# Loading batch 0 in 1 KB pieces and batch 1 ahead of the weights, with queries left in piece order

## The chip, the cores and the metric

One core of one Trainium2 chip. The metric is the device time of one execution in microseconds (us). The kernel before takes 378.52 us, the median of 3 runs (378.29 to 378.92). "Faster" and "slower" need 2%.

## The reference

```python
# q, k, v: 8 batches x 8 heads x 576 rows x 64 columns, fp32; s: 8 x 8 x 576
scores = scale * q @ k.T
bias   = -(cum[..., :, None] - cum[..., None, :])        # cum = cumsum(max(s, 0))
scores = where(causal, -1e9, scores + minimum(bias, 0))
x      = softmax(scores) @ v            # heads side by side: 8 x 576 x 512
xn     = (x - mean) / sqrt(var + 1e-6) * g_ln
out    = x + maximum(xn @ w_ch1, 0) @ w_ch2              # 512 -> 2048 -> 512
```

## The kernel before

A hand-scheduled loop over 64 heads. Head g's scores, exponentials and products with v lie beside the transposes of later heads and beside pieces ("units") of the MLP of an earlier batch. The parts that matter here:

```python
QUADS = (1, 2)                 # batches whose q and k are loaded in 1 KB pieces
ypool = ctx.enter_context(tc.tile_pool(name="ypool", bufs=2))   # output tiles yo
...
def head_in(what, b, h, eng):          # loads of batches 0 to 2, one head each
    o, i = homes[what, b][:, h, 0:NF, :], src[what][b, h, 0 : NF * P, :]
    if b in QUADS and what != "v":     # partition p gets rows 4p to 4p+3: 1 KB
        eng.dma_start(out=o.rearrange("p t d -> p (t d)"),
                      in_=i.rearrange("(p t) d -> p (t d)", t=NF))
    else:                              # partition p gets rows p, 128+p, ...: 4 x 256 B
        eng.dma_start(out=o, in_=i.rearrange("(t p) d -> p t d", p=P))
...
def t_quads(b, h, engs):               # transposes on TensorE, then a copy out of PSUM
    ...                                # that puts the columns back in row order, q and k
        copy(engs[i], qkT[b][0:DK, i * H + h, 0 : NF * P].rearrange("r (p t) -> r p t", t=NF),
             pts[i][0:DK, 0 : NF * P].rearrange("r (t p) -> r p t", t=NF))
...
late.append((out[c, a * P : (a + 1) * P, :], yo))      # a store of 128 rows x 2 KB
...
for c, g in enumerate((6, 6, 7, 7)):             at(g, "a", lambda c=c: load_w1(c))
for h, g in enumerate((0, 0, 1, 1, 7, 7, 8, 8)): at(g, "e", lambda h=h: b1_in(h))
for i, g in enumerate((10, 10, 11, 11)):         at(g, "b", lambda i=i: load_w2(i))
```

From batch 3 on, q and k are transposed by DMA instead (`t_dma`, tile qkT: 25 transposes, a median of 5.5 us from issue to landing in the kernel before). The page counts the packets of all queues as shares of 16 DMA engines: 63.5% of the span for queue q1, with the loads, 6.3% for q10, with most of the stores.

The softmax here doesn't subtract the row's maximum and nothing guards it: scores larger than these inputs give would overflow.

Of the kernel before, what the change touches and what calls it, by code (L numbers as in the profile page):

```python
# [9 lines left out]
F32 = mybir.dt.float32  # L10
BF16 = mybir.dt.bfloat16
# [5 lines left out]
def kernel(  # L17
# [35 lines left out]

    QUADS = (1, 2)
    NPX = 2
# [17 lines left out]

    negm = const.tile([P, P], BF16, name="negm")
    nc.gpsimd.memset(negm, 0.0)
    nc.gpsimd.affine_select(
        out=negm, in_=negm, compare_op=ALU.is_ge, fill=-131072.0, base=0, pattern=[[1, P]],
        channel_multiplier=-1,
    )

# [16 lines left out]
    xnT_tail = const.tile([P, 2, KD, P], BF16, name="xnT_tail")  # L97

    scr = xbufs[0]
    ident_f = scr[:BH, 4:5, 64 : 64 + BH].rearrange("p a b -> p (a b)")  # L100
# [4 lines left out]

    nc.sync.dma_start(out=s_sb, in_=s.rearrange("b h s -> (b h) s"))


# [12 lines left out]
    def copy(eng, o, i):  # L121
        if eng == "act":
            nc.scalar.copy(out=o, in_=i)
        elif eng == "dve":
            nc.vector.tensor_copy(out=o, in_=i)  # L125
        else:
            nc.gpsimd.tensor_copy(out=o, in_=i)  # L127
# [33 lines left out]
    def t_quads(b, h, engs):  # L161
        pts = [ps_m.tile([P, 2 * 512], BF16, name="pt", tag="pm") for _ in range(2)]
        tails = pts[1][0:DK, NF * P : NF * P + 2 * P].rearrange("r (j n) -> r j n", j=2)
        for i in range(2):
            for p in range(NF):
                nc.tensor.transpose(  # L166
                    pts[i][0:DK, p * P : (p + 1) * P], aug[:, p, i * H + h, 0:DK], ident
                )
            nc.tensor.transpose(tails[:, i, :], aug[:, NF, i * H + h, 0:DK], ident)
            copy(  # L170
                engs[i],
                qkT[b][0:DK, i * H + h, 0 : NF * P].rearrange("r (p t) -> r p t", t=NF),
                pts[i][0:DK, 0 : NF * P].rearrange("r (t p) -> r p t", t=NF),
            )
        copy(
            "dve", qkT[b][0:DK, :, NF * P : S].rearrange("r (j h) n -> r j h n", j=2)[:, :, h, :],
            tails[:, :, 0:TL],
        )

    def t_pe(b, h, engs=("dve", "dve")):  # L180
        if b in QUADS:
            return t_quads(b, h, engs)
        for j, eng in ((h, engs[0]), (H + h, engs[1])):
            pt = ps_m.tile([P, 2 * 512], BF16, name="pt", tag="pm")
            for p in range(NT):
                nc.tensor.transpose(pt[0:DK, p * P : (p + 1) * P], aug[:, p, j, 0:DK], ident)  # L186
            copy(eng, qkT[b][0:DK, j, :], pt[0:DK, 0:SP_])

# [9 lines left out]
    def score_mms(g):  # L198
        b, h = g // H, g % H
        s01 = ps_s.tile([P, 1024], F32, name="s01", tag="s01")  # L200
        s23 = ps_s.tile([P, 512], F32, name="s23", tag="s23")
        pot = ps_o.tile([P, 512], F32, name="pot", tag="pot")
        pots[g] = (pot, s01, s23)

        def mm(o, kb, lo, hi):
            lhsT = qkT[b][0:DK, H + h, kb * P : (kb + 1) * P]
            w = 0
            if g < NPM and lo == kb * P:
                w = min(P, hi - lo)
                nc.tensor.matmul(  # L210
                    o[:, 0:w], lhsT=lhsT, rhs=qkT[b][0:DK, h, lo : lo + w], start=True, stop=False
                )
                nc.tensor.matmul(
                    o[:, 0:w], lhsT=ident, rhs=negm[:, 0:w], start=False, stop=True
                )
            if lo + w < hi:
                nc.tensor.matmul(  # L217
                    o[:, w:], lhsT=lhsT, rhs=qkT[b][0:DK, h, lo + w : hi], start=True, stop=True
                )

        mm(s01[:, 0:512], 0, 0, 512)
        mm(s01[:, 512:576], 0, 512, 576)
        mm(s01[:, 576:1024], 1, 128, 576)
        mm(s23[:, 0:320], 2, 256, 576)
        mm(s23[:, 320:512], 3, 384, 576)
        mm(pot[:, 448:512], 4, 512, 576)

    def score_exp(g, part):
        pot, s01, s23 = pots[g]
        e = ebufs[g % 3]  # L230

        def ex(o, i):
            nc.scalar.activation(out=o, in_=i, func=ACT.Exp, scale=scale)  # L233

        def mask(d):
            nc.gpsimd.affine_select(  # L236
                out=d, in_=d, compare_op=ALU.is_ge, fill=0.0, base=0,
                pattern=[[0, d.shape[1]], [1, P]], channel_multiplier=-1,
            )

        if part == 0:
            ex(e[:, 0:1024], s01)
        else:
            ex(e[:, EO[2] : EO[2] + 512], s23)
            ex(e[:, EO[4] : EO[4] + TL], pot[:, 448:512])
            if g >= NPM:
                mask(e[:, 0 : 3 * S].rearrange("p (n c) -> p n c", c=S)[:, :, 0:P])
                mask(
                    e[:, EO[4] + P - 448 : EO[3] + P]
                    .rearrange("p (n c) -> p n c", c=448)[:, :, 448 - P : 448]  # L250
                )

# [39 lines left out]
    def store(c, a, yo):  # L292
        if c >= B:
            b0 = 4 * (c - B) + 2 * a
            late.append((out[b0, NF * P : S, :], yo[0:TL]))
            late.append((out[b0 + 1, NF * P : S, :], yo[TL:P]))
        else:
            late.append((out[c, a * P : (a + 1) * P, :], yo))

# [190 lines left out]
    def spin(n):  # L490
        for _ in range(n):
            nc.tensor.matmul(idle[:, 0:P], lhsT=ident, rhs=ident, start=True, stop=True)

    spin(44)
    nc.vector.tensor_scalar(
# [5 lines left out]
    )  # L501
    pc = ps_m.tile([P, 512], F32, name="pc", tag="pm")
    for p in range(NT):
        nc.tensor.transpose(pc[:, p * BH : (p + 1) * BH], cum[:, p * P : (p + 1) * P], ident_f)
    c8, r8 = (
        x[:, 0 : NT * BH].rearrange("p (t c) -> p t c", c=BH) for x in (xts[2], xts[1])
    )
    pc_v = pc[:, 0 : NT * BH].rearrange("p (t c) -> p t c", c=BH)

# [11 lines left out]
    cast_head("k", 0, 0, "pool")  # L521
    split(0, H, nc.vector, pc_v[:, :, 0:H], aug[:, :, H:HD, D1:DK])
    nc.scalar.activation(
# [3 lines left out]
    cast_head("k", 0, 1, "pool")  # L527
    spin(8)
    t_pe(0, 0, ("act", "dve"))
    nc.scalar.copy(out=c8, in_=pc_v)  # L530

    def cum_quads():

        pq = ps_m.tile([P, 512], F32, name="pq", tag="pm")[:, 0 : NF * 3 * H]
        pq = pq.rearrange("p (t c) -> p t c", t=NF)
        cum_q = cum[0 : 3 * H, 0 : NF * P].rearrange("c (p t) -> c t p", t=NF)
        for p in range(NF):
            nc.tensor.transpose(pq[:, p, :], cum_q[:, p, :], ident_f[0 : 3 * H, 0 : 3 * H])
        qs = slice(QUADS[0] * H, (QUADS[-1] + 1) * H)
        nc.vector.tensor_copy(out=c8[:, 0:NF, qs], in_=pq[:, :, qs])  # L540

# [10 lines left out]
    def at(g, pos, f):  # L552
        hooks.setdefault((g, pos), []).append(f)
# [13 lines left out]
    def t_next(g):  # L567
        t_pe((g + 2) // H, (g + 2) % H, ("dve", "act" if g >= H else "dve"))

    at(0, "a2", lambda: t_pe(0, 1))  # L570
    at(0, "a2", cum_quads)
    at(2, "c", lambda: split(H, 2 * H, nc.vector))
# [3 lines left out]
    for g in range(2 * H):  # L576
        if g < 12:
            at(g, "a", lambda g=g: feed(g))
        if g < 14:
            at(g, "a2" if g < H else "b", lambda g=g: t_next(g))  # L580
    for c, g in enumerate((6, 6, 7, 7)):
        at(g, "a", lambda c=c: load_w1(c))

    def heads_in(b, hs):
        for h in hs:
            for what in "qkv":
                head_in(what, b, h, nc.sync)

    def b1_in(h):
        if h == 2:  # L590
            nc.sync.dma_start(out=gln_b, in_=moe_g_ln.partition_broadcast(P))
        heads_in(1, (h,))
        if h % HH == 0:
            for what in "qkv":
                tails_in(what, 1, nc.sync, slice(h, h + HH))

    for h, g in enumerate((0, 0, 1, 1, 7, 7, 8, 8)):
        at(g, "e", lambda h=h: b1_in(h))
# [6 lines left out]
    def t_act(b, h):  # L605
        t_pe(b, h, ("dve", "act"))

# [18 lines left out]
    at(10, "c", lambda: chunk_units(0))  # L626
    for i, g in enumerate((10, 10, 11, 11)):
        at(g, "b", lambda i=i: load_w2(i))
    for p in (1, 2, 3, 4):
        at(6 + p, "e", lambda p=p: nc.gpsimd.memset(aug[:, p, :, DK:P], 0.0))  # L630


    def b2_in(g):
        if g == 12:
            for what in "qkv":
                tails_in(what, 2, nc.sync)
        heads_in(2, range(3 * (g - 12), min(H, 3 * (g - 12) + 3)))

    for g in (12, 13, 14):
        at(g, "a", lambda g=g: b2_in(g))  # L640
# [62 lines left out]
    for g in range(NG + 4):  # L703
# [7 lines left out]
        if g < NG:  # L711
            score_mms(g)
            run(g, "a2")
            score_exp(g, 0)
        mlp(min(1, nu))
# [44 lines left out]
```

## Time and profile before

| kernel before | value |
|---|---|
| time, median | 378.52 us |
| span of the profiled execution (its own time was 380.23 us) | 378.5 us |
| idle time of TensorE from 98.8 to 320 us | 0.8 us (221.20 less 220.41) |
| data of one store of batches 0 to 2, first packet to last, median of 12 (range) | 1.4 us (0.8 to 2.6) |

```profile
DVE x L273 <- DMA out_dram<-yo: 0.5, 1, 0.5
```

### The profile page before, as it was taken

The numbers are of one execution on the slowest core, as the hardware profiler recorded it, in microseconds if no ns is written. First come the engines' busy times: TensorE is split into PE (matmuls) and PEld (weight loads), VectorE is DVE, ScalarE is ACT, GpSimd is POOL, SyncE is SP. The second block draws the span as 40 slices with busy tenths as digits, with TensorE's granted clock in tenths as the row PEclk, the third lists the DMA queues.
The fourth block names the chain that finished last, engine by engine and source line by source line (L and its number), as shares of the span: only waits on it lengthen the run. The fifth ranks groups of instructions, "written<-read, shape, count | busy, mean of one in ns | idle before, by whom it ended". The sixth has DMA issues, their size and how long they took to land.

```text
span 378.5 us, 7931 instructions
## 1 busy us (share of the span) xinstructions
PE 354.7 (94%) x3017; PEld 204.5 (54%) x3017; DVE 201.9 (53%) x466; ACT 163.9 (43%) x295; POOL 167.6 (44%) x328
## 2 busy tenths in 40 slices
PE   6987878888999999999999999999999999899994
PEld 5966645455555455545555755555555555344471
DVE  6788575765454544594447435733555353933131
ACT  3755755154563457335632546444623554031020
POOL 3537964493634545575455544463444111500000
PEclk9998999999999999999999999999999999999998
DMA  9958989997999789999999999599804001420202
GB/s 164 207 150 190 221 143 187 245 248 176 176 227 227 137 198 211 229 198 205 174 210 239 174 246 224 119 195 207 156 29 113 29 2 55 113 55 0 86 28 55
DMA packets 175253, 59.12 MB, mean 156 GB/s; under 512 B 162224, under 2 KB 170416, under 8 KB 175216
## 3 DMA queue, kind: packets, MB, share of 16 engines
q1 hardware_dynamic: 165200, 46.43, 63.5%
q0 software_dynamic: 4224, 4.19, 7.0%
q10 hardware_dynamic: 5792, 8.00, 6.3%
q8 instruction: 23, 0.38, 0.4%
q14 instruction: 14, 0.11, 0.1%
HBM read 37.11 MB, written 9.44 MB: 123 GB/s over the span
## 4 chain that ended last, share of the span: by engine, by line
PE 75%; DMA 11%; DVE 6%; SPq 4%; issue 2%; POOL 1%; ACT 0%; DVEq 0%; POOLq 0%; ACTq 0%
PE ph L373 29%; PE py L384 28%; PE s L217 9%; PE pot L264 6%; DMA ring<-in_q_dram 4%; DMA ring<-in_v_dram 4%; DVE xn L323 2%; SPq L430 2%; DMA ring<-in_k_dram 1%; DVE stats L308 1%; DMA xnT<-xn 1%; SPq L422 1%; SPq L434 1%; DVE x L273 1%; PE pt L186 1%
## 5 line engine op out<-in xcount | busy, mean ns | idle before, releaser
L233 ACT ACTIVATE e<-s 128x1024 bf16<-128x1024 f32 (+1 forms) x128 | 99.0, 808 | 88.0 <-PE s L217 86.2
L384 PE MATMUL py<-w_bf,hT 128*128 128x512 bf16 x576 | 133.4, 379 | 0.0
L373 PE MATMUL ph<-xnT,w_bf 128*128 128x512 bf16 x512 | 120.7, 379 | 1.7 <-DMA xnT<-xn 1.7
L236 POOL TENSOR_SCALAR_AFFINE_SELECT e<-e 128x384 bf16<-128x384 bf16 x104 | 45.7, 464 | 111.2 <-ACT e L233 102.6
L358 DVE TENSOR_SCALAR hT<-ph 128x512 bf16<-128x512 f32 x72 | 49.6, 690 | 77.0 <-PE ph L373 76.4
L373 PEld LDWEIGHTS <-w_bf 128*128 128x128 bf16 x640 | 58.2, 98 | 50.3 <-issue 2.2
L384 PEld LDWEIGHTS <-hT 128*128 128x128 bf16 x576 | 53.1, 98 | 56.1 <-DVE hT L358 0.2
L356 ACT ACTIVATE hT<-ph 128x512 bf16<-128x512 f32 x72 | 43.0, 597 | 79.6 <-PE ph L373 77.3
L217 PE MATMUL s<-qkT 68*128 68x64 bf16 (+5 forms) x320 | 54.5, 287 | 0.0
L127 POOL CAST aug<-ring 128x512 bf16<-128x512 f32 (+2 forms) x85 | 44.4, 547 | 15.0 <-DMA ring<-in_k_dram 7.3
L390 DVE SCALAR_TENSOR_TENSOR yo<-py,rstd,x 128x512 f32<-128x512 f32 x32 | 24.0, 749 | 47.7 <-PE py L384 45.5
L217 PEld LDWEIGHTS <-qkT 68*128 68x128 bf16 x372 | 32.5, 98 | 24.7
L264 PEld LDWEIGHTS <-e 128*128 128x128 bf16 x960 | 37.9, 98 | 13.6 <-POOL e L236 1.1
L264 PE MATMUL pot<-v_bf,e 128*128 128x65 bf16 x960 | 40.1, 194 | 1.4 <-POOL e L236 1.0
L273 DVE TENSOR_TENSOR x<-pot,rinv 128x320 f32<-128x320 f32 x64 | 31.5, 492 | 2.9 <-DMA out_dram<-yo 0.5
L125 DVE COPY qkT<-pt 68x512 bf16<-68x512 bf16 (+2 forms) x49 | 21.9, 468 | 12.5 <-PE pt L166 4.4
L308 DVE BATCH_NORM_STATS2 stats<-x 128x6 f32<-128x256 f32 (+2 forms) x68 | 23.4, 398 | 0.3
L323 DVE SCALAR_TENSOR_TENSOR xn<-x,mv,gln_b 128x512 bf16<-128x512 f32 x32 | 23.2, 766 | 0.0
L127 POOL CAST v_bf<-ring 128x512 bf16<-128x512 f32 (+2 forms) x33 | 19.5, 613 | 2.2 <-DMA ring<-in_v_dram 2.2
L272 DVE RECIPROCAL rinv<-pot 128x5 f32<-128x5 f32 x64 | 12.0, 187 | 15.0 <-PE pot L264 14.9
L329 POOL TENSOR_TENSOR rstd<-rstd,nhalf 128x2 f32<-128x2 f32 x18 | 18.6, 1031 | 1.5
L166 PE MATMUL pt<-ident,aug 128*68 128x128 bf16 x128 | 11.8, 226 | 6.8 <-POOL aug L127 3.1
(78 smaller groups left out, 217.8 us busy)
## 6 DMA issues: line engine op xcount, KB each, us to landing
out_dram<-yo ACTq DMA_DIRECT2D x27, 256.0 KB, 3.3
ring<-in_q_dram SPq DMA_DIRECT2D x20, 256.0 KB, 4.9
ring<-in_k_dram SPq DMA_DIRECT2D x20, 256.0 KB, 4.8
ring<-in_v_dram SPq DMA_DIRECT2D x20, 256.0 KB, 4.3
w_bf<-in_moe_w_ch_dram POOLq DMA_DIRECT2D x8, 512.0 KB, 9.7
ring<-in_k_dram SPq DMA_DIRECT2D x30, 128.0 KB, 4.2
ring<-in_q_dram SPq DMA_DIRECT2D x22, 128.0 KB, 4.7
x<-in_v_dram SPq DMA_DIRECT2D x17, 128.0 KB, 4.0
```

The source lines that it names most:

```text
L127: nc.gpsimd.tensor_copy(out=o, in_=i)
L217: nc.tensor.matmul(o[:, w:], lhsT=lhsT, rhs=qkT[b][0:DK, h, lo + w : hi], start=True, stop=True)
L233: nc.scalar.activation(out=o, in_=i, func=ACT.Exp, scale=scale)
L236: nc.gpsimd.affine_select(out=d, in_=d, compare_op=ALU.is_ge, fill=0.0, base=0, pattern=[[0, d.shape[1]], [1, P]], channel_multiplier=-1,)
L264: nc.tensor.matmul(pot[:, t * D1 : (t + 1) * D1], lhsT=e[:, c : c + P], rhs=v_bfs[b % 2][:, kb, h, :], start=(kb == 0), stop=(kb == t),)
L273: nc.vector.tensor_tensor(out=xs[b][:, :, h * D : (h + 1) * D], in0=pv[:, :, 0:D], in1=rv.to_broadcast([P, NT, D]), op=ALU.mult,)
L308: nc.vector.bn_stats(out=sts[c, a][:, part, :], in_=x_of(c, a)[:, lo:hi])
L323: eng.scalar_tensor_tensor(out=xn[:, j, :], in0=x_of(c, a), scalar=mv[:, j, 0:1], in1=gln_b, op0=ALU.subtract, op1=ALU.mult,)
L356: nc.scalar.activation(out=o, in_=i, func=ACT.Relu)
L358: nc.vector.tensor_scalar_max(out=o, in0=i, scalar1=0.0)
L373: nc.tensor.matmul(ph[:, j * tok : (j + 1) * tok], lhsT=w1_bf[:, kd, fb * P : (fb + 1) * P], rhs=xnT[c][:, :, kd, :], start=(kd == 0), sto ...
L384: nc.tensor.matmul(st["py"], lhsT=st["h"][:, fb, a * P : (a + 1) * P], rhs=w2_bf[:, fb, :], start=(fb == 0), stop=(fb == FB - 1),)
```

## The change

Its intent: the first 95 us have holes on TensorE while transfers are busy. Bigger packets for batch 0 free transfer time early (in the trace of the kernel before a packet of 256 bytes took 21.1 ns, one of 1 KB 55.2); batch 1 whole ahead of W1 and W2 (the weights w_ch1 and w_ch2) ends the waits for its casts in heads 7 to 10. To save VectorE a reordering copy, the queries stay in piece order (row 4q+t at place 32t+q of each block of 128); the masks follow that order, and the store puts the rows right.

```diff
-    QUADS = (1, 2)
+    QUADS = (0, 1, 2)
+    QN, QP = 4, 32
 ...  t_quads: queries are copied as they are, keys still put in row order
+            if i == 0:
+                copy(engs[0], o[:, 0:S], pt[0:DK, 0:S])
+            else:
+                copy(engs[1], o[:, 0 : NF * P].rearrange("r (p t) -> r p t", t=NF), ...)
+                copy(engs[2], o[:, NF * P : S], pt[0:DK, NF * P : S])
 ...  score matmuls read the block's queries as 4 runs of 32 columns
+                qT = qT[:, 0 : NF * P].rearrange("r (t a p) -> r a t p", t=QN, p=QP)
 ...  the store
-            late.append((out[c, a * P : (a + 1) * P, :], yo))
+            o = out[c, a * P : (a + 1) * P, :]
+            if c in QUADS:
+                o = o.rearrange("(q t) f -> t q f", t=QN)
+            late.append((o, yo))
 ...  order of loads
-    for c, g in enumerate((6, 6, 7, 7)):             # W1
+    for c, g in enumerate((7, 7, 8, 8)):
-    for h, g in enumerate((0, 0, 1, 1, 7, 7, 8, 8)): # batch 1
+    for h, g in enumerate((1, 1, 1, 1, 3, 3, 3, 3)):
-    for i, g in enumerate((10, 10, 11, 11)):         # W2
+    for i, g in enumerate((9, 9, 10, 10)):
 ...  cut: masks in piece order; g spread by a TensorE product with ones instead of a
 ...  broadcast load; warm-up of 11 matmuls of 512 columns for 44 of 128; the last score
 ...  tile queued after the next head's transposes; cumulative sums in two steps
```

More of the change, by code (lines that the diff above doesn't have):

```diff
@@ L71 @@
     make_identity(nc, ident)
-    negm = const.tile([P, P], BF16, name="negm")
-    nc.gpsimd.memset(negm, 0.0)
-    nc.gpsimd.affine_select(
-        out=negm, in_=negm, compare_op=ALU.is_ge, fill=-131072.0, base=0, pattern=[[1, P]],
-        channel_multiplier=-1,
-    )
+    negm = const.tile([P, TL], BF16, name="negm")
+    negq = const.tile([P, P], BF16, name="negq")
+    for m, pattern in ((negq, [[1, QN], [QN, QP]]), (negm, [[1, TL]])):
+        nc.gpsimd.memset(m, 0.0)
+        nc.gpsimd.affine_select(
+            out=m, in_=m, compare_op=ALU.is_ge, fill=-131072.0, base=0, pattern=pattern,
+            channel_multiplier=-1,
+        )
     ctx.enter_context(tc.manual_schedule())
@@ L97 @@
     xnT_tail = const.tile([P, 2, KD, P], BF16, name="xnT_tail")
+    gln_r, ones_r = xts[0][0:1, :], xts[2][0:1, Dm - P : Dm]
     scr = xbufs[0]
@@ L106 @@
     nc.sync.dma_start(out=s_sb, in_=s.rearrange("b h s -> (b h) s"))
+    nc.gpsimd.dma_start(out=gln_r, in_=moe_g_ln.rearrange("(o f) -> o f", o=1))
+    nc.gpsimd.memset(ones_r, 1.0)
     staged = {}
@@ L161, in t_quads @@
     def t_quads(b, h, engs):
-        pts = [ps_m.tile([P, 2 * 512], BF16, name="pt", tag="pm") for _ in range(2)]
-        tails = pts[1][0:DK, NF * P : NF * P + 2 * P].rearrange("r (j n) -> r j n", j=2)
         for i in range(2):
-            for p in range(NF):
+            pt = ps_m.tile([P, 2 * 512], BF16, name="pt", tag="pm")
+            o = qkT[b][0:DK, i * H + h, :]
+            for p in range(NT):
                 nc.tensor.transpose(
-                    pts[i][0:DK, p * P : (p + 1) * P], aug[:, p, i * H + h, 0:DK], ident
+                    pt[0:DK, p * P : (p + 1) * P], aug[:, p, i * H + h, 0:DK], ident
                 )
-            nc.tensor.transpose(tails[:, i, :], aug[:, NF, i * H + h, 0:DK], ident)
-            copy(
-                engs[i],
-                qkT[b][0:DK, i * H + h, 0 : NF * P].rearrange("r (p t) -> r p t", t=NF),
-                pts[i][0:DK, 0 : NF * P].rearrange("r (t p) -> r p t", t=NF),
-            )
-        copy(
-            "dve", qkT[b][0:DK, :, NF * P : S].rearrange("r (j h) n -> r j h n", j=2)[:, :, h, :],
-            tails[:, :, 0:TL],
-        )
-    def t_pe(b, h, engs=("dve", "dve")):
-        if b in QUADS:
-            return t_quads(b, h, engs)
-        for j, eng in ((h, engs[0]), (H + h, engs[1])):
-            pt = ps_m.tile([P, 2 * 512], BF16, name="pt", tag="pm")
-            for p in range(NT):
-                nc.tensor.transpose(pt[0:DK, p * P : (p + 1) * P], aug[:, p, j, 0:DK], ident)
-            copy(eng, qkT[b][0:DK, j, :], pt[0:DK, 0:SP_])
+            if i == 0:
+                copy(engs[0], o[:, 0:S], pt[0:DK, 0:S])
+            else:
+                copy(
+                    engs[1], o[:, 0 : NF * P].rearrange("r (p t) -> r p t", t=NF),
+                    pt[0:DK, 0 : NF * P].rearrange("r (t p) -> r p t", t=NF),
+                )
+                copy(engs[2], o[:, NF * P : S], pt[0:DK, NF * P : S])
     def t_dma(b, p):
@@ L203, in score_mms, with queries @@
         pots[g] = (pot, s01, s23)
+        def queries(lo, hi):
+            qT = qkT[b][0:DK, h, :]
+            if b in QUADS and hi <= NF * P:
+                qT = qT[:, 0 : NF * P].rearrange("r (t a p) -> r a t p", t=QN, p=QP)
+                return qT[:, lo // P : hi // P]
+            return qT[:, lo:hi]
         def mm(o, kb, lo, hi):
             lhsT = qkT[b][0:DK, H + h, kb * P : (kb + 1) * P]
-            w = 0
+            cuts = {lo, hi}
+            if b in QUADS and lo < NF * P:
+                cuts.add(min(hi, NF * P))
             if g < NPM and lo == kb * P:
-                w = min(P, hi - lo)
-                nc.tensor.matmul(
-                    o[:, 0:w], lhsT=lhsT, rhs=qkT[b][0:DK, h, lo : lo + w], start=True, stop=False
-                )
-                nc.tensor.matmul(
-                    o[:, 0:w], lhsT=ident, rhs=negm[:, 0:w], start=False, stop=True
-                )
-            if lo + w < hi:
-                nc.tensor.matmul(
-                    o[:, w:], lhsT=lhsT, rhs=qkT[b][0:DK, h, lo + w : hi], start=True, stop=True
-                )
+                cuts.add(min(hi, lo + P))
+            cuts = sorted(cuts)
+            for c0, c1 in zip(cuts[:-1], cuts[1:]):
+                d = o[:, c0 - lo : c1 - lo]
+                m = g < NPM and c0 == kb * P
+                nc.tensor.matmul(d, lhsT=lhsT, rhs=queries(c0, c1), start=True, stop=not m)
+                if m:
+                    nc.tensor.matmul(
+                        d, lhsT=ident,
+                        rhs=(negq if b in QUADS and kb < NF else negm)[:, 0 : c1 - c0],
+                        start=False, stop=True,
+                    )
         mm(s01[:, 0:512], 0, 0, 512)
@@ L225, in score_mms @@
         mm(s23[:, 320:512], 3, 384, 576)
-        mm(pot[:, 448:512], 4, 512, 576)
+        return lambda: mm(pot[:, 448:512], 4, 512, 576)
     def score_exp(g, part):
@@ L235, in mask @@
         def mask(d):
+            n, w = d.shape[1], d.shape[2]
+            pattern = [[0, n], [1, w]]
+            if g // H in QUADS and w == P:
+                d = d.rearrange("p n (t q) -> p n t q", t=QN)
+                pattern = [[0, n], [1, QN], [QN, QP]]
             nc.gpsimd.affine_select(
-                out=d, in_=d, compare_op=ALU.is_ge, fill=0.0, base=0,
-                pattern=[[0, d.shape[1]], [1, P]], channel_multiplier=-1,
+                out=d, in_=d, compare_op=ALU.is_ge, fill=0.0, base=0, pattern=pattern,
+                channel_multiplier=-1,
             )
@@ L247, in score_exp @@
                 mask(e[:, 0 : 3 * S].rearrange("p (n c) -> p n c", c=S)[:, :, 0:P])
-                mask(
-                    e[:, EO[4] + P - 448 : EO[3] + P]
-                    .rearrange("p (n c) -> p n c", c=448)[:, :, 448 - P : 448]
-                )
+                if g // H in QUADS:
+                    for c, w in ((EO[3], P), (EO[4], TL)):
+                        mask(e[:, c : c + w].rearrange("p (n c) -> p n c", n=1))
+                else:
+                    mask(
+                        e[:, EO[4] + P - 448 : EO[3] + P]
+                        .rearrange("p (n c) -> p n c", c=448)[:, :, 448 - P : 448]
+                    )
     xs = {}
@@ L491, in spin @@
         for _ in range(n):
-            nc.tensor.matmul(idle[:, 0:P], lhsT=ident, rhs=ident, start=True, stop=True)
-    spin(44)
+            nc.tensor.matmul(
+                idle, lhsT=ident,
+                rhs=ident.rearrange("p (o n) -> p o n", o=1).to_broadcast([P, 4, P]),
+                start=True, stop=True,
+            )
+    spin(11)
     nc.vector.tensor_scalar(
@@ L501 @@
     )
-    pc = ps_m.tile([P, 512], F32, name="pc", tag="pm")
+    NQ = len(QUADS) * H
+    pq = ps_m.tile([P, 512], F32, name="pq", tag="pm")[:, 0 : NT * NQ]
+    pq = pq.rearrange("p (t c) -> p t c", t=NT)
+    cum_q = cum[0:NQ, 0 : NF * P].rearrange("c (p t) -> c t p", t=NF)
     for p in range(NT):
-        nc.tensor.transpose(pc[:, p * BH : (p + 1) * BH], cum[:, p * P : (p + 1) * P], ident_f)
+        nc.tensor.transpose(
+            pq[:, p, :], cum_q[:, p, :] if p < NF else cum[0:NQ, NF * P : SP_],
+            ident_f[0:NQ, 0:NQ],
+        )
     c8, r8 = (
@@ L507 @@
     )
-    pc_v = pc[:, 0 : NT * BH].rearrange("p (t c) -> p t c", c=BH)
     def split(lo, hi, eng, a=None, o=None):
@@ L521 @@
     cast_head("k", 0, 0, "pool")
-    split(0, H, nc.vector, pc_v[:, :, 0:H], aug[:, :, H:HD, D1:DK])
+    split(0, H, nc.vector, pq[:, :, 0:H], aug[:, :, H:HD, D1:DK])
     nc.scalar.activation(
@@ L527, with cum_all, spread_g @@
     cast_head("k", 0, 1, "pool")
-    spin(8)
-    t_pe(0, 0, ("act", "dve"))
-    nc.scalar.copy(out=c8, in_=pc_v)
-    def cum_quads():
-        pq = ps_m.tile([P, 512], F32, name="pq", tag="pm")[:, 0 : NF * 3 * H]
-        pq = pq.rearrange("p (t c) -> p t c", t=NF)
-        cum_q = cum[0 : 3 * H, 0 : NF * P].rearrange("c (p t) -> c t p", t=NF)
-        for p in range(NF):
-            nc.tensor.transpose(pq[:, p, :], cum_q[:, p, :], ident_f[0 : 3 * H, 0 : 3 * H])
-        qs = slice(QUADS[0] * H, (QUADS[-1] + 1) * H)
-        nc.vector.tensor_copy(out=c8[:, 0:NF, qs], in_=pq[:, :, qs])
+    spin(2)
+    t_quads(0, 0, ("act", "dve", "act"))
+    nc.scalar.copy(out=c8[:, :, 0:NQ], in_=pq)
+    def cum_all():
+        pc = ps_m.tile([P, 512], F32, name="pc", tag="pm")
+        pc_v = pc[:, 0 : NT * BH].rearrange("p (t c) -> p t c", c=BH)
+        for p in range(NT):
+            nc.tensor.transpose(pc_v[:, p, :], cum[:, p * P : (p + 1) * P], ident_f)
+        nc.vector.tensor_copy(out=c8[:, :, NQ:BH], in_=pc_v[:, :, NQ:BH])
+    def spread_g():
+        pg = ps_m.tile([P, 512], F32, name="pg", tag="pm")
+        nc.tensor.matmul(pg, lhsT=ones_r, rhs=gln_r, start=True, stop=True)
+        nc.vector.tensor_copy(out=gln_b, in_=pg)
     cast_head("q", 0, 2, "dve")
@@ L567, in t_next @@
     def t_next(g):
-        t_pe((g + 2) // H, (g + 2) % H, ("dve", "act" if g >= H else "dve"))
-    at(0, "a2", lambda: t_pe(0, 1))
-    at(0, "a2", cum_quads)
+        t_quads((g + 2) // H, (g + 2) % H, ("dve", "act" if g >= H else "dve", "dve"))
+    at(0, "a2", lambda: t_quads(0, 1, ("dve", "dve", "dve")))
+    at(1, "c", cum_all)
+    at(3, "c", spread_g)
     at(2, "c", lambda: split(H, 2 * H, nc.vector))
@@ L589, in b1_in @@
     def b1_in(h):
-        if h == 2:
-            nc.sync.dma_start(out=gln_b, in_=moe_g_ln.partition_broadcast(P))
         heads_in(1, (h,))
@@ L605, in t_act @@
     def t_act(b, h):
-        t_pe(b, h, ("dve", "act"))
+        t_quads(b, h, ("dve", "act", "dve"))
     def c_head(b, h):
@@ L630 @@
         at(6 + p, "e", lambda p=p: nc.gpsimd.memset(aug[:, p, :, DK:P], 0.0))
+    B2 = 12
     def b2_in(g):
-        if g == 12:
+        if g == B2:
             for what in "qkv":
                 tails_in(what, 2, nc.sync)
-        heads_in(2, range(3 * (g - 12), min(H, 3 * (g - 12) + 3)))
-    for g in (12, 13, 14):
+        heads_in(2, range(3 * (g - B2), min(H, 3 * (g - B2) + 3)))
+    for g in (B2, B2 + 1, B2 + 2):
         at(g, "a", lambda g=g: b2_in(g))
@@ L711 @@
         if g < NG:
-            score_mms(g)
+            score_tail = score_mms(g)
             run(g, "a2")
+            score_tail()
             score_exp(g, 0)
```

## The prediction

> **What bounds the kernel now.** I read the page's slices and its chain first, then busy time by stretch, then TensorE's waits by stretch, then the chain in order of time over the first 71 us.
>
> The page: engines' busy tenths in 40 slices of 9.5 us, and the chain of waits by engine.
>
> ```profile
> PE   6987878888999999999999999999999999899994
> DVE  6788575765454544594447435733555353933131
> ACT  3755755154563457335632546444623554031020
> POOL 3537964493634545575455544463444111500000
> PEclk9998999999999999999999999999999999999998
> DMA  9958989997999789999999999599804001420202
> ...
> PE 75%; DMA 11%; DVE 6%; SPq 4%; issue 2%; POOL 1%; ACT 0%; DVEq 0%; POOLq 0%; ACTq 0%
> ```
>
> From the eleventh slice to the 34th TensorE is full. Only the first ten slices (95 us: batches 0 and 1 and the start of the MLP) and the tail have holes, and transfers are busy in those ten slices. So only work or waits before about 95 us can gain; what is saved there reaches the end whole if the full stretch after it does not change.
>
> Busy time by stretch; I cut at the starts of head 0 (9.36), head 7 (27.05), head 11 (43.00), head 16 (80.4), head 19 (98.8), read off the timeline of score matmuls.
>
> ```profile
> 9.36:27.05 17.69, 16.10 (x279) 14.15 (x279) 13.60 (x38) 11.67 (x22) 8.28 (x19) 1.00 0.85 176
> 27.05:43.00 15.95, 12.09 (x183) 10.10 (x180) 12.99 (x37) 9.35 (x18) 12.82 (x22) 0.89 0.98 201
> 43.00:80.40 37.40, 31.37 (x290) 18.22 (x288) 23.65 (x52) 18.18 (x33) 24.11 (x48) 1.00 1.00 201
> 80.40:98.80 18.40, 17.04 (x160) 10.44 (x158) 10.09 (x22) 9.32 (x17) 10.62 (x26) 1.00 0.89 196
> 98.80:320.00 221.20, 220.41 (x1771) 119.78 (x1770) 112.41 (x255) 105.46 (x190) 102.80 (x196) 1.00 0.85 166
> ```
>
> Columns: length, busy us of PE, PEld, DVE, ACT, POOL, granted clock, DMA share, GB/s. Heads 7 to 10 take 15.95 us with 12.09 busy, at a granted clock of 0.89. That is the worst stretch.
>
> Who TensorE waited for between 24 and 43 us, then the longest pieces of the chain up to 71 us:
>
> ```profile
> PE pt L166 <- POOL aug L127: 3.1, 5, 1.3
> PE pot L210 <- POOL aug L127: 0.5, 1, 0.5
> PE ptx L340 <- ACT xnT L123: 0.5, 1, 0.5
> PE pot L264 <- POOL v_bf L127: 0.4, 1, 0.4
> PE pot L210 <- DVE x L273: 0.4, 1, 0.4
> ```
>
> ```profile
> 26.93 5.11 DMA ring<-in_k_dram
> ...
> 37.46 14.17 DMA ring<-in_v_dram
> ...
> 61.32 9.03 DMA ring<-in_q_dram
> ```
>
> TensorE waits for GpSimd's casts, and these wait for batch 1's pieces. A v piece issued at 37.46 lands 14.17 us later, in the middle of the four W1 loads (GpSimd issues them at 32.99 to 37.9). The second half of batch 1 and W1 are under way together.
>
> [...] in its packet records a 256-byte packet took 21.1 ns at 9.4 to 19.4 us, a 1 KB packet 55.2 ns at 19.4 to 26.4 us, so four times the bytes for 2.6 times the time. [...] The changed stores of batches 0 to 2 have an output pattern of 4 x 32 x 512[...]. No transfer of the kernel before has such a pattern[...]. [...] the clock is 0.50 from 35.2 to 38.6 us, right after a window (31.8 to 35.2) with 2.17 us busy of 3.40.
>
> **The change part by part.** Group means are from the costliest groups of instructions.
>
> *Batch 0's q and k in 1 KB pieces.* 8192 packets of 21.1 ns become 2048 of 55.2 ns: 10.8 us of the 16 engines become 7.1 us, 3.7 us less. Batch 0 should have landed at about 17 us instead of 21. TensorE needs about 2.13 us a head here (heads 3 to 4) and mostly isn't waiting for data, so little of it is gained in batch 0 itself: the first head was held by ScalarE's cast of q head 1, landed at 8.17 us, and scores started at 9.36. Without that wait they start when VectorE has copied k, at about 9.0: 0.35 us.
>
> *Batch 0 pays for it.* The k copy scatters: 681 ns for 512 columns where 640 plain columns took 481. The q copy stays plain (estimate 430), the 64-column tail adds about 130. VectorE per head: 430+660+130+190+490 = 1.9 us, before 2x445+680 = 1.6. Added on VectorE in heads 1 to 5: the copies of the whole cumulative sum and of g, about 1.0 us together. TensorE gets two small matmuls more a head (cuts at 512), net 0.03 us each[...]. The second set of cumulative-sum transposes (0.58) moves from head 0 to head 1. So head 7 starts at about 26.8 instead of 27.05: nearly nothing won.
>
> *Batch 1 whole, ahead of the weights.* Batch 1 needs, at the packet times above, about 15 us of the engines (7.1 for q and k, 5.4 for v, 2 for tails); started at 17 us, it has landed at about 33 us instead of 51.7. W1 then runs alone and is there at about 45 us (both weights: 7.0% of the span, so 13 us each), W2 at 58 us, batch 2 by about 73 us. First uses, by my walk: head 11 for W1, 16 units later for W2, head 16 for batch 2. None late. In heads 7 to 10 this removes 3.1+0.5+0.4 = 4.0 us of waits for casts and probably the half clock (3.4 us at half: at most 1.7, with its own waits about 1.3). But these heads then meet other limits: VectorE has 10 us of work in heads 7 to 9 (copies 0.54 to 1.2, output 0.67, statistics 2.0, the four xn at 766 each with their aggregations 3.6) against 6.9 of TensorE, and ScalarE 2.32 a head plus 2.13 of xnT copies in head 10. Walking VectorE's queue I get a wait of about 1.6 us in head 10 that was not there. Head 11's first MLP matmul starts at 40.0 instead of 44.09. Gain by then 4.1 us, the 0.35 included.
>
> *Heads 11 to 18.* The wait of 0.96 for a mask behind W2's issue goes, since W2 is issued two heads earlier. The 9.03 us landing of batch 2's q goes off the chain: 0.99 for xn and some 0.3 more. Not removed: 1.95 us behind the split of the cumulative sum on VectorE (it stays in head 12), and about 2 us of latency in batch 1's norm. Gain 2.2.
>
> *Added on TensorE where it is full.* Three more matmuls a head from head 12 to 23, 0.1 us a head: 1.2 us lost.
>
> *Masks.* In heads 12 to 23 three instructions for two: 0.1 us a head on GpSimd, which waits for ScalarE there. Nothing.
>
> *Last score tile later.* Two waits of 0.4 us for VectorE's output, in heads 4 and 6, fall behind the transposes. Used up by VectorE's longer queue.
>
> *Stores on 4 engines.* 32 packets of 2 KB each at 88 ns: 2.8 us instead of 0.7, about double beside loads. Twelve stores. By the times of the 4 outputs of a chunk, a buffer is needed 3.3 us after its store is issued in the closest case (batch 1's last), else 6 us or more. I take 0.4 us.
>
> Sum: 4.1 + 2.2 - 1.2 - 0.4 = 4.7 us. Predicted 378.5 - 4.7 = 373.8 us.
>
> **The rivals.** *VectorE takes over wholly.* For it: its busy share in heads 7 to 10 is already 12.99 of 15.95, and there is more of it. If its instructions stretch[...], heads 7 to 10 keep 2 to 3 us of their waits: 376 to 377. *All waits go.* Against it: the waits from 43 to 99 us are mostly VectorE's (1.9, 1.8, 1.0, 0.9). If they were shifts of the late data after all, the gain would be 8 to 9 us: 370. *The transfers are the bound anyway.* DMA share is near 1.0 up to 98 us. If 1 KB packets gain nothing beside the weights, W1 comes late, and the wait moves to head 11: 376. *The narrow stores hurt.* If loads behind them are held up by 3 us twelve times, the casts of batch 3 and later wait. Against it: after 100 us GpSimd never waited for a transfer, and the ring is ten tiles deep. If wrong, 376 to 379.
>
> **Range and chances.** The weak terms are VectorE's walk (plus or minus 1.5 us), the clock (1.3), and the stores (minus 2). I say 370.8 to 377.2. Faster by over 2% means under 370.95: 0.12. Slower by over 2% would need the stores and VectorE both to go wrong and more: 0.02. Within 2%: 0.86.
>
> **What would show it.** Right: casts of batch 1 no longer wait for transfers after about 27 us; the last v piece lands before 38; the clock has no half stretch near 35; head 7 starts within 0.5 us of 27; the first MLP matmul at 39 to 41.5; from there to head 16 about 2 us less than 36.3; from 100 to 320 the order of work as before. TensorE's waits in heads 7 to 10 name VectorE. Wrong: head 7 well before 25.5 or after 28.5; a wait for W1 at head 11; stores spread over less than 4 us with loads beside them, or VectorE waiting for stores for over 2 us in all; TensorE holes after 100 us.

## More of the kernel before

Stores are issued from ScalarE's queue, loads and transposes from SyncE's.

The two lines here are TensorE's longest wait after 100 us and VectorE's one wait for a store between 60 and 240 us (columns: us in total, times, longest).

```profile
PE ph L373 <- DMA xnT<-xn: 1.7, 1, 1.7
```

## The result, and the profile after

The changed kernel takes 395.69 us (4 runs: 399.24, 396.79, 393.9, 394.58), against 378.72 for the kernel before beside it: ratio 1.0461, 95% interval 1.0382 to 1.0539. It is slower. The profiled execution is the slowest of the four, 399.24, with a span of 397.5; its loss is 19.0 us in the spans, where the medians differ by 17.0.

The page of the changed kernel: TensorE's busy tenths and its granted clock in 40 slices of 9.9 us, and the chain by engine and by line.

```profile
PE   7997989879997699839999799999999999989995
...
PEclk9899999999998999968999899999999999999999
...
PE 60%; DMA 12%; DVE 2%; issue 1%; POOL 1%; SPq 1%; ACT 0%; ACTq 0%; DVEq 0%
PE ph L392 28%; PE py L403 20%; PE s L220 7%; DMA qkT<-aug 6%; PE pot L280 4%; DMA out_dram<-yo 4%; DMA xnT<-xn 1%; DVE yo L409 1%; DVE xn L342 1%; SPq L124 1%; ACT e L240 0%; POOL v_bf L135 0%; PE ptx L359 0%; DVE stats L327 0%; PE pot L220 0%
```

The stretch that was full has holes: the 13th and 14th slices (119 to 139 us) have 7 and 6, the 18th (169 to 179 us) has 3, at a granted clock of 6 tenths, and the 23rd has 7. Two kinds of transfer are on the chain: stores (4%) and the transposes of q and k (6%). Busy time by stretch of the changed kernel, cut at head 7, head 11, head 16 and head 19, then the two worst later stretches and the rest (columns as in the prediction):

```profile
26.60:42.70 16.10, 13.01 (x228) 12.03 (x226) 13.73 (x43) 11.60 (x23) 15.54 (x29) 0.89 1.05 203
42.70:76.00 33.30, 30.68 (x295) 18.18 (x295) 21.23 (x52) 17.64 (x33) 21.12 (x45) 1.00 1.11 219
76.00:94.65 18.65, 16.33 (x159) 10.19 (x160) 8.14 (x21) 8.87 (x17) 10.37 (x27) 1.00 0.75 157
...
120.00:141.00 21.00, 15.23 (x87) 7.73 (x87) 6.24 (x13) 6.60 (x12) 7.46 (x14) 0.84 0.61 148
...
165.00:182.00 17.00, 9.11 (x32) 3.68 (x31) 7.23 (x18) 1.63 (x3) 5.46 (x9) 0.70 0.95 131
182.00:320.00 138.00, 134.59 (x1065) 73.97 (x1075) 65.96 (x148) 61.76 (x111) 63.11 (x119) 0.99 0.87 163
```

Head 19's scores start at 94.64 us instead of 98.81: the front did win 4.17 us. After that point the changed kernel needs 302.9 us (397.5 less 94.64) where the kernel before needs 279.7: 23.2 us lost. TensorE idles 5.8 us in the stretch from 120 us, 7.9 in that from 165 and 3.4 from 182 to 320; and it works 15.5 us at half clock after 100 us (in four half-clock stretches found in the clock's records), which costs about half of that, 7.8 us (an estimate: in the longest of them, from 171.41 us, the 12 matmuls of L403 kept TensorE busy for 5.4 us, 0.45 each, where from 226.1 to 300 us, at full clock, 98 of them took 23.6, 0.24 each). With the few tenths idle in between, that is about 25 us against 0.8 before, enough for the loss of 23.2.

What TensorE waited for after 100 us in the changed kernel, and below it what VectorE waited for from 60 to 240 us:

```profile
PE s L220 <- DMA qkT<-aug: 10.5, 2, 7.7
PE ph L392 <- DVE yo L409: 3.1, 1, 3.1
PE ptx L359 <- DVE yo L409: 2.5, 1, 2.5
PE ph L392 <- DMA xnT<-xn: 1.9, 1, 1.9
```

```profile
DVE yo L409 <- DMA out_dram<-yo: 25.1, 7, 6.5
```

VectorE waits seven times for an output buffer whose store is not done: 25.1 us where the kernel before has 0.5. TensorE then waits for VectorE's yo, and scores wait for transposes. The longest pieces of the chain, in order of time (start, length):

```profile
114.75 7.91 DMA out_dram<-yo
...
128.40 8.57 DMA out_dram<-yo
...
160.19 15.08 DMA qkT<-aug
...
211.43 10.12 DMA qkT<-aug
```

On the chain a store is done some 8 us after its issue. A transpose issued at 160.19 lands 15.08 us later; two stores were issued beside it, at 160.7 and 162.2 us. Of these 15.08 us the issue alone took 8.93 on SyncE's queue, where the longest issue of such a transpose in the kernel before took 4.97. In the packet records one narrow store (one with the output pattern 4 x 32 x 512) takes 5.5 us from first to last packet (median of 12, 3.8 to 6.9), where the kernel before has 1.4. These records do not name the engines. On the stores' queue there are 544 packets of 4 bytes in the kernel before, 16 for each of its 34 transfers, and 400 in the changed kernel, 12 fewer for each of the twelve stores: 4 each. Of the 2 KB packets of one such store 2.0 to 3.6 are under way at once on average, where the kernel before has 4.3 to 14.6. That fits 4 engines instead of 16, which is my estimate from these counts.

### The profile page after: what moved, and what is told of

Its sections match the earlier page's. It is cut to its first block, busy times and chain, and to the rows that moved or that the text cites. A ratio compares the mean times of both kernels' runs of the same rounds, so it can differ in the third digit from the quotient of the medians. Undisturbed runs are those within 1.5% of the kernel's fastest.

```text
span 397.5 us, 7984 instructions
## 1 busy us (share of the span) xinstructions
PE 362.4 (91%) x3014; PEld 207.4 (52%) x3041; DVE 198.9 (50%) x474; ACT 163.6 (41%) x296; POOL 171.5 (43%) x345
## 4 chain that ended last, share of the span: by engine, by line
PE 60%; DMA 12%; DVE 2%; issue 1%; POOL 1%; SPq 1%; ACT 0%; ACTq 0%; DVEq 0%
PE ph L392 28%; PE py L403 20%; PE s L220 7%; DMA qkT<-aug 6%; PE pot L280 4%; DMA out_dram<-yo 4%; DMA xnT<-xn 1%; DVE yo L409 1%; DVE xn L342 1%; SPq L124 1%; ACT e L240 0%; POOL v_bf L135 0%; PE ptx L359 0%; DVE stats L327 0%; PE pot L220 0%
## 5 line engine op out<-in xcount | busy, mean ns | idle before, releaser
L403 PE MATMUL py<-w_bf,hT 128*128 128x512 bf16 x549 | 134.5, 389 | 1.7 <-issue 0.4
L392 PE MATMUL ph<-xnT,w_bf 128*128 128x512 bf16 x512 | 122.1, 382 | 5.0 <-DVE yo L409 3.1
L248 POOL TENSOR_SCALAR_AFFINE_SELECT e<-e 128x384 bf16<-128x384 bf16 (+2 forms) x116 | 48.7, 444 | 119.4 <-ACT e L240 111.0
L403 PEld LDWEIGHTS <-hT 128*128 128x128 bf16 x576 | 54.3, 100 | 59.2 <-issue 5.5
L220 PE MATMUL s<-qkT 68*128 68x64 bf16 (+7 forms) x428 | 56.9, 264 | 11.3 <-DMA qkT<-aug 10.5
L220 PEld LDWEIGHTS <-qkT 68*128 68x128 bf16 x492 | 40.4, 99 | 41.7 <-issue 12.7
L133 DVE COPY qkT<-pt 68x576 bf16<-68x576 bf16 (+2 forms) x56 | 19.6, 380 | 12.9 <-PE pt L174 7.6
L174 PE MATMUL pt<-ident,aug 128*68 128x128 bf16 x240 | 19.3, 230 | 3.7 <-DVE yo L409 1.5
L135 POOL CAST v_bf<-ring 128x512 bf16<-128x512 f32 (+2 forms) x33 | 18.3, 577 | 4.1 <-DMA ring<-in_v_dram 4.1
L174 PEld LDWEIGHTS <-aug 128*68 128x68 bf16 x240 | 16.2, 119 | 6.5 <-issue 3.8
L347 POOL TENSOR_SCALAR rstd<-mv 128x2 f32<-128x2 f32 x18 | 10.4, 577 | 20.8 <-DVE mv L338 20.7
```

Source lines behind the costliest of these rows:

```text
L135: nc.gpsimd.tensor_copy(out=o, in_=i)
L174: nc.tensor.transpose(pt[0:DK, p * P : (p + 1) * P], aug[:, p, i * H + h, 0:DK], ident)
L220: nc.tensor.matmul(d, lhsT=lhsT, rhs=queries(c0, c1), start=True, stop=not m)
L248: nc.gpsimd.affine_select(out=d, in_=d, compare_op=ALU.is_ge, fill=0.0, base=0, pattern=pattern, channel_multiplier=-1,)
L392: nc.tensor.matmul(ph[:, j * tok : (j + 1) * tok], lhsT=w1_bf[:, kd, fb * P : (fb + 1) * P], rhs=xnT[c][:, :, kd, :], start=(kd == 0), sto ...
L403: nc.tensor.matmul(st["py"], lhsT=st["h"][:, fb, a * P : (a + 1) * P], rhs=w2_bf[:, fb, :], start=(fb == 0), stop=(fb == FB - 1),)
```

## The experiments

Theory: the stores of batches 0 to 2, on few DMA engines, are the whole loss; the rest of the change gains some 5 us. Rival 1: the added matmuls, masks and copies, or the new order of loads, lose the time later. Rival 2: it is the scattered rows of those stores, not the count of outer rows (the size of the slowest dimension of the store's output pattern). Unless said otherwise, the kernel before beside the runs took 378.81 us (first four runs), 378.39 (next four), 378.24 (next three) and 378.57 (the last).

### Only the pattern of the stores: 16 or 8 outer rows, and narrow stores in the kernel before

These three write rows to wrong places on purpose; sizes and bytes are the same.

```diff
  changed kernel, 16 outer rows (and with t=8 in the other run):
-                o = o.rearrange("(q t) f -> t q f", t=QN)
+                o = o.rearrange("(q t) f -> t q f", t=16)
  kernel before, narrow stores and nothing else:
+            if c < 3:
+                o = o.rearrange("(q t) f -> t q f", t=4)
```

> The changed kernel, one store each, same bytes and 2 KB rows, but the output pattern 16 x 8 x 512 instead of 4 x 32 x 512 (rows land in a wrong order, on purpose). Theory 1 [...] 372 to 376 us. Theory 2, or a cost of strided rows as such: 388 us or more.

> The same with 8 x 16 x 512 (wrong order on purpose)[...]. Theory 1: between, 374 to 382 us, with stores of about 1.4 us alone and VectorE waiting for stores under 8 us in all. Theory 2: 388 us or more.

> The kernel before with only its stores of batches 0 to 2 put into the 4 x 32 x 512 pattern (wrong order on purpose). Theory 1: 392 to 402 us, that is the same 15 to 20 us that the changed kernel loses after 100 us. Theory 2: 378 to 381 us.

Measured:

| kernel | outer rows | data of one store, median | VectorE's wait for stores, 60 to 240 us | time | ratio (95%) |
|---|---|---|---|---|---|
| changed | 4 | 5.5 us | 25.1 us | 395.69 | 1.0461 (1.0382 to 1.0539) |
| changed | 8 | 3.2 us | 7.2 us | 380.68 | 1.0004 (0.9911 to 1.0096) |
| changed | 16 | 2.2 us | 4.6 us | 373.13 | 0.9891 (0.9827 to 0.9956) |
| before | 128 (natural) | 1.4 us | 0.5 us | 378.7 | 1 |
| before | 4 | 5.0 us | 19.9 us | 396.9 | 1.0488 (1.0464 to 1.0512) |

With 16 outer rows the changed kernel takes 373.13 us (372.95 to 378.11; the profiled execution is the slowest, 378.11, and its wait of 4.6 us belongs to that). The kernel before with narrow stores alone loses 18 us, with no other part of the change in it. Its profile shows the same waits, of VectorE from 60 to 240 us and of TensorE after 100 us; the third line is the stretch where its clock was at half.

```profile
DVE yo L393 <- DMA out_dram<-yo: 19.9, 6, 7.9
```

```profile
PE ph L376 <- DMA xnT<-xn: 9.6, 2, 7.8
PE s L217 <- DMA qkT<-aug: 2.7, 1, 2.7
PE ptx L343 <- DVE yo L393: 2.6, 1, 2.6
PE ph L376 <- DVE yo L393: 2.5, 1, 2.5
```

```profile
179.32:189.56 10.24, 4.64 (x13) 1.81 (x14) 3.35 (x6) 0.72 (x2) 0.72 (x2) 0.50 1.36 151
```

So taking the narrow pattern away from the changed kernel wins 22.6 us, and putting it into the kernel before costs 18. Rival 1 falls. The time follows the outer rows, 16, 8, 4, in order, though the intervals of 16 and 8 overlap. The packets of 4 bytes on the stores' queue follow them too: 544 with 16, 448 with 8 and 400 with 4, so 0, 8 and 12 fewer a store, which fits 16, 8 and 4 engines (an estimate, as above).

### Scattered rows alone

```diff
  kernel before:
+            if c < 3:
+                o = o.rearrange("(q t) f -> t q f", t=16)
```

> Control: the kernel before, stores of batches 0 to 2 in the pattern 16 x 8 rows (wrong row order on purpose). If only the count of outer rows matters and scattered rows by themselves cost nothing: same as before, 378 to 380 us, VectorE's wait for stores under 1 us. If scattered rows themselves cost: over 381 us.

Measured: 377.74 us (377.36 to 378.64), ratio 0.999 (0.9952 to 1.0027), and no wait of VectorE for a store from 60 to 240 us. Scattered rows by themselves cost nothing that shows; rival 2 falls. (Wrong row order.)

### Four stores of 32 partitions for one

```diff
-                o = o.rearrange("(q t) f -> t q f", t=QN)
-            late.append((o, yo))
+                late.append([(o[t], yo[t * QP : (t + 1) * QP]) for t in range(QN)])   # 4 DMAs
```

> The changed kernel with each store of batches 0 to 2 as four stores of 32 partitions (result right). Theory 1, stores confined to 4 of the 16 transfer engines hold up transposes and output buffers after 100 us: 374 to 377 us (four times the issues on ScalarE cost a little), VectorE's wait for stores from 25.1 us to under 3, no wait of TensorE for qkT. Theory 2, the loss is from the reordered loads and VectorE's new work, stores are only where it shows: 388 us or more.

Measured: correct, 383.44 us (381.7 to 384.58), ratio 1.0128 (1.0091 to 1.0166). A miss: 12 us better than the changed kernel, but 10 us worse than with one store of 16 outer rows. TensorE's waits for qkT after 100 us are gone, as forecast, but VectorE still waits 17.2 us for stores, not under 3: so much waiting of VectorE can stand beside a far smaller loss. ScalarE's waits from 100 to 320 us point to a new cost, which no run isolates:

```profile
ACT xnT L131 <- DMA out_dram<-yo: 8.6, 1, 8.6
...
ACT e L240 <- DMA out_dram<-yo: 6.4, 2, 5.3
ACT e L240 <- DMA ring<-in_k_dram: 4.6, 1, 4.6
```

ScalarE, which issues the stores, stood up to 8.6 us until older transfers had landed, with its exponentials behind (up to 5.3 us); in the kernel before it waits for no transfer in that stretch. Why it waits is not shown. I had counted engines alone.

### The queries put back in row order by TensorE's operand

```diff
-                qT = qT[:, 0 : NF * P].rearrange("r (t a p) -> r a t p", t=QN, p=QP)
-                return qT[:, lo // P : hi // P]
+                return qT[:, 0 : NF * P].rearrange("r (t p) -> r p t", t=QN)[:, lo // QN : hi // QN]
  and masks and stores as in the kernel before
```

> The changed kernel, but the queries are put back in natural row order by TensorE itself: the moving operand of each score matmul is read with a step of 128 columns, so outputs, masks and stores are natural again and no store has 4 outer rows. Correct result. If the narrow stores are the whole loss and the stepped operand costs TensorE nothing: 371 to 375 us, VectorE's waits for stores in batches 0 to 2 under 1 us, the mean of a score matmul in heads 12 to 23 as in the kernel before. If the stepped operand costs TensorE time (rival): score matmuls of those heads longer by a few per cent each, 376 us or more. If the loss had another source than the stores: near 395 us.

Measured: correct, 414.09 us (408.86 to 416.8), ratio 1.0901 (1.0816 to 1.0986). The rival of this run was right, and by far more than it said. Score matmuls from 43 to 96 us in this kernel, and after them the one group of the kernel before that compares (last number before the second bar: mean ns of one):

```profile
L218 PE MATMUL s<-qkT 68*128 68x384 bf16 x9 | 7.3, 811 | 0.0
L218 PE MATMUL s<-qkT 68*128 68x512 bf16 x4 | 4.1, 1028 | 0.0
```

```profile
L217 PE MATMUL s<-qkT 68*128 68x512 bf16 x7 | 2.7, 381 | 0.0
```

A moving operand read with a step of 256 bytes (four steps, then back to the next column) takes 1028 ns for 512 columns instead of 381, both at full clock. Not all of the loss need be this: the clock of the profiled execution was also at half from 9.4 to 36.7 us. The changed kernel's own reading, in runs of 32 columns, took 381 ns for 512 as well, so that part of the change costs a score matmul nothing. The same kernel with the old order of the loads:

> The kernel of the run with naturally ordered queries, with the old order of the loads (batch 1 split in two with W1 between, W1 and W2 as before). If the new load order carries the gain of the front: back to 377 to 380 us, first MLP matmul near 44 us. If the 1 KB pieces of batch 0 carry it: 372 to 375 us, first MLP matmul near 40 to 42 us.

Measured: 417.19 us (415.98 to 418.42). Its result is wrong: batch 1's q is then loaded over the cumulative sums before they have all been read (with that reading moved from head 1 to head 0, the old order gives a right result in a run below). The stepped operand hides what this run was for, so it says little.

### The queries put back in row order by the copy

```diff
  changed kernel, with t_quads of the kernel before (both copies reorder), natural masks and stores:
-                copy(engs[0], o[:, 0:S], pt[0:DK, 0:S])
+            copy(engs[i], qkT[b][0:DK, i * H + h, 0 : NF * P].rearrange("r (p t) -> r p t", t=NF),
+                 pts[i][0:DK, 0 : NF * P].rearrange("r (t p) -> r p t", t=NF))
```

> The changed kernel with one part undone: the queries of batches 0 to 2 are put in row order by the copy out of PSUM (as the kernel before does for batches 1 and 2), so stores, masks and score matmuls are natural again; everything else of the change stays. Correct result. If the loss was the narrow stores alone: 372 to 376 us, score matmuls of 512 columns near 381 ns, VectorE's waits for stores under 1 us; the reordering copy is about 0.23 us longer than the contiguous one, eight of them in the heads where VectorE bounds, so up to 2 us above the 373.1 us of the run with 16 outer rows. If something else of the change hurts: 380 us or more.

Measured: correct, 376.09 us (372.62 to 376.4, 6 runs), ratio 0.9905 (0.9861 to 0.995). With two variants below, which do not differ from it clear of noise (375.95 and 376.11 us), it is the fastest kernel here with a right result, 1% ahead of the kernel before, which is not "faster" at 2%. No wait of VectorE for a store is left from 60 to 240 us, and score matmuls of 512 columns take 381 ns again. Four of its six runs took 375.8 to 376.4 us at a mean granted clock of 0.986 to 0.990, and two 372.6 and 373.2 at 0.997 and 0.998. Busy time by 4 us in one of the four, the profiled one of 376.4:

```profile
30.00:34.00 4.00, 3.28 (x60) 2.80 (x57) 3.86 (x14) 2.75 (x5) 3.44 (x8) 1.00 1.12 190
34.00:38.00 4.00, 2.52 (x50) 2.26 (x49) 3.91 (x15) 3.10 (x7) 3.69 (x6) 1.00 1.20 214
38.00:42.00 4.00, 3.06 (x44) 2.76 (x42) 2.60 (x6) 2.67 (x6) 3.84 (x7) 0.69 1.20 223
42.00:46.00 4.00, 4.00 (x19) 1.91 (x18) 0.00 (x0) 2.21 (x5) 2.66 (x5) 0.50 1.20 225
```

VectorE is busy all of 34 to 38 us, TensorE 2.52 of 4, and then the clock is at half for 6.8 us, until 46.4. That costs at most half of it, 3.4 us, which is about what lies between the two groups. That the stretch makes the difference is not shown, and one trace speaks against it: the same kernel with the old warm-up, below, took 375.94 us in its profiled execution with full clock from 5.0 to 325.8 us. Nor do the eleven runs of the kernel before beside these sort by clock (379.32 us at 0.998, 376.78 at 0.989).

### The order of the loads, the pieces, the warm-up

```diff
  kernel before, new order alone: batch 1 at heads 1,1,1,1,3,3,3,3; W1 at 7,7,8,8; W2 at 9,9,10,10
  reordering copies, old order:   batch 1 at heads 0,0,1,1,7,7,8,8; W1 at 6,6,7,7; W2 at 10,10,11,11;
                                  and all cumulative sums read in head 0 instead of head 1
  reordering copies, old warm-up: 44 and 8 matmuls of 128 columns for 11 and 2 of 512
```

> The kernel before with the new load order alone (batch 1 whole ahead of the weights), batch 0 still in 256-byte pieces. Theory (order carries the front gain): first MLP matmul near 41 us, 374 to 376 us. Rival (needs the 1 KB pieces of batch 0, since batch 1 now queues behind a slower batch 0): VectorE and GpSimd casts of batch 1 wait for their loads, first MLP matmul 43 us or later, 377 to 380 us.

> The run with reordering copies, with the old order of the loads (batch 1 in two halves with W1 between), so of the front only the 1 KB pieces of batch 0 are left. The order alone, in the kernel before, gave 1.7 us. If pieces and order add up: near 375.5 to 377.5 us. If the pieces carry nearly all of the gain: within 1 us of the run with the new order. If the pieces are worth nothing without the order: 378 us or more.

> The same with the warm-up of the kernel before (44 and 8 matmuls of 128 columns in place of 11 and 2 of 512). If the later full clock of the changed kernel (7.6 us against 4.5) is due to the wider spin matmuls: full clock near 4.5 us again, head 0's scores under 9.5 us, and 0.3 to 1 us faster than the run without it. Rival: no difference, because the casts and loads of head 0 set its start.

Measured: order alone 376.66 us, ratio 0.9955 (0.9918 to 0.9991); all but the order 376.98, ratio 0.9956 (0.9926 to 0.9986); both 0.9905, as above. Each by itself gives about 0.45%, both about 0.95%, so they seem to add; the intervals overlap, so that is not shown. The order alone gave less than I expected (374 to 376), though its first MLP matmul came at 41.5 us, as forecast: where the waits for GpSimd's casts were, TensorE now waits for VectorE, from 27 to 43 us of that run:

```profile
PE pot L210 <- DVE x L273: 3.6, 3, 1.9
```

The warm-up makes no difference that is clear of noise: 375.95 us, ratio 0.9921 (0.9886 to 0.9956). Head 0's scores start at 9.5 us with either, and the first full clock comes at 5.0 us with the old one and 5.4 with the new.

### ScalarE takes query copies from VectorE

```diff
  kernel with reordering copies:
-        t_quads(..., ("dve", "act" if g >= H else "dve", "dve"))
+        t_quads(..., ("act" if 3 <= g < H else "dve", "act" if g >= H else "dve", "dve"))
```

> The kernel with reordering copies, where from head 3's turn to head 7's the query copy (about 0.68 us on VectorE) goes to ScalarE (about 0.58 us), which had about 1.3 us free of every 4 there: VectorE is busy 3.9 of every 4 us from 18 to 38 us, so it is the limit of those heads. If so: VectorE falls to about 3.2 of 4 us, TensorE's wait for the values' products (3.1 us in that stretch) shrinks by half or more, the half-clock stretch near 40 us is gone in most executions, and the time is 372 to 374.5 us against 376.1. Rival: GpSimd (3.7 to 4.0 of 4 us there) or the loads take the limit over at once: no difference, 375.5 to 376.5 us.

Measured: correct, 376.11 us (374.98 to 377.94), ratio 0.9924 (0.9903 to 0.9946): no difference, the rival was right. Busy time in this kernel:

```profile
26.00:30.00 4.00, 3.26 (x58) 2.95 (x58) 3.03 (x9) 2.59 (x6) 4.00 (x9) 1.00 0.75 191
30.00:34.00 4.00, 3.26 (x70) 2.99 (x68) 3.23 (x9) 3.56 (x7) 3.60 (x7) 1.00 1.09 179
...
38.00:42.00 4.00, 1.85 (x35) 1.73 (x36) 3.87 (x12) 2.38 (x5) 4.00 (x7) 0.92 1.21 223
42.00:46.00 4.00, 4.00 (x30) 2.85 (x28) 0.34 (x1) 2.59 (x4) 3.84 (x8) 0.50 1.20 238
```

VectorE fell from 3.9 to between 2.5 and 3.3 of 4 us from 22 to 38 us, but it is at 3.87 again from 38 to 42. GpSimd is busy 4.00 of 4 in two of these stretches, TensorE has its hole at 38 to 42 us all the same, and the clock is still halved. So taking work from VectorE alone did not help; which limit takes over is argued from these shares and not shown.

## Why the prediction was wrong

I predicted 373.8 us, 370.8 to 377.2, and gave "slower by over 2%" a chance of 0.02. It is 395.69, and slower.

**The step that failed is "Stores on 4 engines. [...] I take 0.4 us."** The term was worth some 20 us: 22.6 from the changed kernel with 16 outer rows (395.69 less 373.13), 18 from the kernel before with narrow stores. Three things in it were wrong, not the first one.
- The count of engines was an assumption then, since no transfer of the kernel before has that pattern. It fits what was measured: 4 packets of 4 bytes a store. The length was right: 2.8 us, "about double beside loads", is 5.6, and 5.5 was measured.
- What was wrong is what I held that length against. I took the buffers as needed 3.3 us after issue at the closest and 6 us or more otherwise. From issue to done a store takes 7.9 and 8.6 us on the chain, since issue and first packet are 1.66 and 2.88 us apart for these two, and a store behind another waits for it: in the packet records three stores in a row (from 125.64, 131.28 and 136.33 us) run back to back, 5.2, 5.1 and 5.0 us each. With two output buffers, the third tile waits. That is VectorE's 25.1 us.
- The rival "the narrow stores hurt" was capped at 379 us because GpSimd never waited for a load. I looked at loads alone; the transposes of q and k and of xn come later too (with narrow stores alone TensorE waited 2.7 us for qkT and 9.6 for xnT), and have no ten tiles of slack. That is TensorE's 10.5 us for qkT.
- Beside the holes on TensorE came work at half clock: 15.5 us of it after 100 us, by my estimate 7.8 us lost. In the 3.41 us before each of its four stretches TensorE was busy for 0.93, 0.93, 0.00 and 1.01 us; that the holes set them off is not shown.

How the loss divides between buffers and transposes stays open: no run here removed one and kept the other (with a third output buffer the program does not build: the buffers ask for 6 KB a partition, and 5 are left). The run with four stores speaks for the transposes without showing it: there VectorE still waited 17.2 us for stores, TensorE not at all for qkT, and 12 of the 22.6 us were won back. Why a transpose is slow beside these stores is open too.

**The other terms came out right in sum, partly by luck.** Without the 0.4 for stores the sum gives 373.4; the changed kernel with 16 outer rows took 373.13. By their own steps, in the profiled execution of the changed kernel:
- Head 0 from 9.36 to about 9.0: wrong, 10.09 in the profiled execution, whose first full clock came at 7.6 us instead of 4.5. With reordering copies it was 9.5 with either warm-up, so the warm-up is not the cause.
- Head 7 at 26.8: right, 26.60, but by luck: the clock was at half from 11.0 to 14.4 us, with TensorE busy all through, which cost up to 1.7 us that I had not foreseen.
- Batch 1 landed at about 33 us, ahead of W1: wrong. SyncE issued its last v piece only at 37.80 us, after W1 (GpSimd issued that from 29.9 to 35.7), and the last packets of batch 1 came at 53.5 us, where the kernel before has 52.3. TensorE's waits for casts in heads 7 to 10 went all the same: from 27 to 46 us GpSimd waited only 0.5 us for transfers, and for the 4.1 us that it waited for v pieces after that, TensorE did not wait.
- First MLP matmul at 40.0: wrong, 42.76, a gain of 1.3 instead of 4.1. TensorE's waits name VectorE, as predicted, but 3.1 us of them instead of 1.6, and the half clock stayed (38.3 to 41.7 us): the rival "VectorE takes over wholly". GpSimd is busy 15.54 of 16.10 us there too.
- Heads 11 to 15: from there to head 16 33.2 us instead of 36.3, a gain of 3.1 where I had 2.2. The two errors partly cancel: 4.17 us at head 19, against 5.6 by my terms up to there (6.3 less 0.7 for the matmuls of heads 12 to 18).
- The 1.2 us for three more matmuls a head and "nothing" for the masks: no run separates them.
- "TensorE holes after 100 us" and "VectorE waiting for stores for over 2 us in all" stood in my list of what would show it wrong. Both came.
- The half clock near 35 us came after a window that was not idle: TensorE was busy for 2.17 of its 3.40 us. Before the two early half-clock stretches of the changed kernel it was busy for 2.12 and 1.74 of 3.41 us. What sets the half clock off is not shown.

## What to carry to other kernels

Before reordering rows in a store, look at the outer rows of its output pattern: 4 of them made each store take 5.5 us instead of 1.4, and with two buffers that cost 5% of the kernel. Reorder where it is cheap (in a copy out of PSUM that is made anyway: 680 ns for 512 reordered columns instead of 447 for 576 plain ones, in the changed kernel), not in the store and not by a stepped operand of TensorE (1028 ns for 512 columns instead of 381). And when a transfer gets slower, ask about every other transfer and about its buffers, from issue to landing (7.9 and 8.6 us here) and not by the length of its data (5.5).
